# Attention, gated MLP and routed experts on one core: where the write of the converted expert weights stands in GpSimd's queue

## The chip, the cores and the metric

The kernel runs on one core of a Trainium2 chip, in one launch. The time is device time in microseconds (us) from the first to the last instruction with what lies around them; 1202.6 us is the median of three runs of the kernel before (1199.43, 1202.60 and 1203.38 us).

## The reference

Three stages in a row. First a two-sided attention, for each of 8 batch items and 8 heads, between 512 text rows `x` and 32 `state` rows of 64 features: softmax(x stateᵀ/8) state, softmax(state xᵀ/8) x. The two results are laid end to end to 8 x 544 = 4352 rows of 512 features. Second a gated MLP over these rows:

```
x = (sigmoid(x @ w_gate) * (x @ w_val)) @ w_out        # 512 -> 1536 -> 512
```

Third a router with 8 experts: each row goes to the expert with the largest logit, `out = p * (relu(x @ w1[e]) @ w2[e])`, 512 -> 1024 -> 512, where p is the softmax probability of that expert.

The MLP's weights arrive as 64-bit floats, the rest as 32-bit floats. The kernel carries a 32-bit value as a pair of 16-bit floats, a high part and a low part (value minus high part), and makes a product of pairs with three matmuls. So every operand has to be scaled by a power of two and split.

## The kernel before, in words

**Stages.** After a prologue (weights converted, attention of the first item) `token_block(b)` runs for the eight batch items b = 0 to 7. Each has a *gated part*: for the 12 feature groups fc of 128, `gate_val` (L657) makes 24 matmuls of 512 columns (L665 to L667; 12 for the gate, 12 for the value), ScalarE takes the sigmoid into the buffer `g` (L671), VectorE multiplies it by the value half (L673), ScalarE casts it to the high part (L678), and GpSimd subtracts to get the low part (L679, "the last subtraction of gated values"). `g` has two buffers, so the sigmoid of group fc+2 has to wait for the subtraction of group fc. The gate and value sums take two of four PSUM buffers for each group. Then comes the *down-projection part*: `mlp_out` for four tiles of 128 rows, 36 matmuls each (L722 to L724). The state rows follow as a ninth block, and then the expert tiles.

**Halves.** Work of other kinds is woven into a block at 36 places, `mid()` (L1153), called halves here: two for each group of the gated part (1 to 24: the odd one between the gate matmuls and the value matmuls, the even one behind the subtraction), three for each tile of the down-projection (25 to 36). At each half `mid()` runs what `todo` lists for it, and in most halves one step of a background generator. What `todo` lists is attention steps of the next item, routing steps, loads, and at halves 24, 26, ... 34 `state_weights(b + 1, m)`: small matmuls (L483) whose result M is taken out of PSUM by ScalarE (L490) and VectorE (L491), twice each.

**The background steps.** From b = 1 to 7 the generator is `conv_experts` (L594). It converts 64 pieces of the experts' weights, 128 x 1024 floats each: load into one of three buffers (L611, SyncE's queue), absolute sum with ScalarE ("bound", L617), spread of that over the partitions with a small matmul (L199, operand `em`), scale (VectorE), split into high and low part by `pair` (high part ScalarE L318, low part VectorE L319) into `out`, a tile with two buffers, and a write of `out` to the DRAM tensor `w_d` (L650), issued on GpSimd's queue. A piece takes three steps: step one is `pair(n)`; step two is the bound of piece n+1 and the write of piece n-1; step three is the load of n+3 and the scale of n+1. Each block runs 28 steps (halves 1 to 24 without every third, and 25 to 36), 196 in all. `pair(n+2)` uses the buffer that the write of piece n empties, and it stands two steps behind that write.

**Order.** The order of PE's instructions is the order of the program text. The order of the other engines' instructions is made ahead of the run by a planner that plays the program through with its own estimates of durations; each engine then runs its queue strictly in that order, whatever the chip's real times. `tc.issue_after(ins)` adds an edge to the plan: instructions of the block that run on the engine of `ins` are placed behind it in that engine's queue. It adds no wait. `behind()` (L217) applies it for the dictionary `last`: `last["A"]` and `last["D"]` are the newest sigmoid or M eviction on ScalarE and the newest multiplication, M eviction or row result on VectorE; `last["P"]` is the newest subtraction L679 on GpSimd, written down but not used.

**Others on GpSimd.** The scatter of routed rows (L825, each waits for the one before to have landed), the low parts of attention (L316), a mask product (L251).

Of the kernel before, what the change touches and what calls it, by code (L numbers as in the profile page):

```python
# [26 lines left out]
def attention_moe_router_kernel(  # L27
# [102 lines left out]
    def tl(shape, dt=F32, name="t", bufs=None, pool=None):  # L130
        kw = {} if bufs is None else {"bufs": bufs}
        return (pool or tiny).tile(shape, dt, name=name, tag=name, **kw)
# [81 lines left out]
    last = {}  # L214

    @contextmanager
    def behind():  # L217

        with ExitStack() as pins:
            for k in "AD":  # L220
                if k in last:
                    pins.enter_context(tc.issue_after(last[k].ins))
            yield

    def state_load(b):

        st = att.tile([P, H // 2, D], F32, name="st", tag="st", bufs=1)
        sv = state[b].rearrange("(c r h) s d -> h s c r d", h=2, c=NU)
        for i in range(2):
            for c in range(NU):  # L230
                for h in range(2):
                    k = 64 * i + NS * (h ^ c)
                    nc.sync.dma_start(out=st[k:k + NS, NP * c:NP * c + NP], in_=sv[h, :, c])
        states[b] = {"st": st}

    def state_max(b):

        g = states[b]
        m = tl([P, 1], name="sgm")
        nc.vector.tensor_reduce(  # L240
            m, g["st"].rearrange("p r d -> p (r d)"), axis=AX.X, op=ALU.max,
            apply_absolute_value=True,
        )
        yield
        r = all_max(spread(m), "sgr")
        g["s"], g["i"] = pow2_scale(r, 14, "sg", bufs=3)

        bf = att.tile([64, H // 2, 2, D], F32, name="bf", tag="a")
        bd = att.tile([64, 2, H // 2, 2, D], F16, name="bd", tag="sT")
        bsh = [64, H // 2, 2, D]  # L250
        nc.gpsimd.tensor_tensor(  # L251
            bf, g["st"][0:64].unsqueeze(2).to_broadcast(bsh),
            hmask[0:64].unsqueeze(3).to_broadcast(bsh), op=ALU.mult,
        )
        bw = bd.rearrange("p l r i d -> p l (r i d)")
        pair(bf.rearrange("p r i d -> p (r i d)"), bw[:, 0], bw[:, 1], g["s"][0:64])
        g["bd"] = bd
        yield

    def state_turn(b):  # L260

        g = states[b]
        bv = g.pop("bd").rearrange("p l r i d -> p l r (i d)")
        pb = at_ps([P, 2, H // 2, 64], F16)
        for l in range(2):
            for r in range(H // 2):
                nc.tensor.transpose(pb[:, l, r], bv[:, l, r], ident[0:64, 0:64])
        g["bdT"] = att.tile([P, 2, H // 2, 64], F16, name="bdT", tag="bdT")
        nc.vector.tensor_copy(g["bdT"], pb)

    def unit_load(n):

        if n >= NUN:
            return
        b, c = divmod(n, NU)
        u = units[n] = {}
        if n == 1:
            u["xb"] = big([P, HU, NJ, D])
        else:
            u["xb"] = att.tile([P, HU, NJ, D], F32, name="xb", tag="xb", bufs=1)  # L280
        for h in range(HU):
            nc.sync.dma_start(
                out=u["xb"][:, h],
                in_=x[b, HU * c + h].rearrange("(p j) d -> p j d", j=NJ),
            )

    def unit_max(n):

        if n >= NUN:
            return  # L290
        u, g = units[n], states[n // NU]
        m = tl([P, 1], name="uxm")

        junk = att.tile([P, NJ * HU * D], F16, name="xj", tag="aq")
        nc.scalar.activation(
            junk, u["xb"].rearrange("p h j d -> p (h j d)"), AF.Abs, accum_out=m
        )
        yield
        r = all_max(spread(m), "uxr")
        u["s"], i = pow2_scale(r, 14, "ux")  # L300

        for nm in ("c1", "c2", "c3", "n1"):
            u[nm] = tl([P, 1], name="s" + nm, bufs=3)
        nc.vector.tensor_scalar(u["c1"], i, g["i"], SCALE, ALU.mult, ALU.mult)
        nc.vector.tensor_scalar(u["n1"], u["c1"], -1.0, None, ALU.mult)
        nc.vector.tensor_scalar(u["c2"], u["c1"], 2.0 ** SC_SH, None, ALU.mult)
        nc.vector.tensor_scalar(u["c3"], i, 2.0 ** -PR_SH, None, ALU.mult)
        yield
# [786 lines left out]
    def token_block(b):  # L1095
        isig = states[b]["i"]
        acts = []
        sg = tl([P, NFC], name="sgf")
        todo = {}

        def at(slot, f):
            todo.setdefault(slot, []).append(f)

        if b + 1 < B:
            if b == 0:
                for u, slots in ((state_max(1), (13, 15)), (unit_max(NU), (14, 16))):
                    for slot in slots:
                        at(slot, lambda u=u: next(u, None))
            at(2 if b else 19, lambda: state_turn(b + 1))

            def first_step(n):
                gens[n] = att_unit(n)
                next(gens[n])

            for c in range(NU):
                n = NU * (b + 1) + c
                slots = (UNIT0, UNIT1)[b][c] if b < 2 else UNIT[c]
                if slots[0]:
                    at(slots[0], lambda n=n: first_step(n))
                for slot in slots[1:]:  # L1120
                    at(slot, lambda n=n: next(gens[n], None))
                if LOAD[min(b, 2)][c]:
                    at(LOAD[min(b, 2)][c], lambda n=n: unit_load(n + 1))
                um = unit_max(n + 1)
                for slot in UMAX[min(b, 2)][c]:
                    at(slot, lambda um=um: next(um, None))
            if 1 <= b < B - 2:
                at(EARLY, lambda: first_step(NU * (b + 2)))
                at(EARLY + 2, lambda: unit_load(NU * (b + 2) + 1))
            for m in range(NFP):  # L1130
                at(GV + 2 * m, lambda m=m: state_weights(b + 1, m))
        if b + 1 == B:
            rs = state_rows()
            at(6, lambda: next(rs, None))
            at(12, lambda: next(rs, None))
        if b + 2 < B:
            at(1 if b else 21, lambda: state_load(b + 2))
            sm = state_max(b + 2)
            at(9 if b else 30, lambda: next(sm, None))
            at(12 if b else 33, lambda: next(sm, None))  # L1140
        if b == 0:

            rw = router_weights()
            for slot in (25, 26, 27, 28, 29, 30, 31, 33):
                at(slot, lambda: next(rw, None))
        for slot in (35, 36) if b == 0 else ROUTE:
            at(slot, lambda: next(router[b], None))
        if b == 1:
            for slot in (3, 6):
                at(slot, lambda: next(router[0], None))  # L1150
        half = [0]

        def mid():  # L1153
            half[0] += 1
            with behind() if b else ExitStack():
                for f in todo.get(half[0], ()):
                    f()
                if half[0] > 12 if b == 0 else half[0] > GV or half[0] % 3:
                    pump(bg)

        if b > 0:
            nc.vector.tensor_scalar(
                sg, inv_w[:, 0], isig, 2.0 ** (M_SH - PR_SH), ALU.mult, ALU.mult
            )
        for fc in range(NFC):
            if b == 0 and fc % 2 == 0:
                fp = fc // 2
                state_weights(0, fp)
                nc.vector.tensor_scalar(
                    sg[:, fc:fc + 2], inv_w[:, 0, fc:fc + 2], isig, 2.0 ** (M_SH - PR_SH),  # L1170
                    ALU.mult, ALU.mult,
                )
                if fp + 2 < NFP:
                    cvs[fp + 2] = conv_wgv(fp + 2, raws.pop(fp + 2))
                    next(cvs[fp + 2])
                    if fp + 3 < NFP:
                        raws[fp + 3] = load_wgv(fp + 3)
            elif b == 0 and fc // 2 + 2 < NFP:
                drain(deque([cvs.pop(fc // 2 + 2)]))
            gate_val(fc, S, sg, V_SH, token_chunks(b, fc), acts, mid)  # L1180
        if b == 0:
            drain(bg)
        rt_new(b, isig)
        router[b] = route(b, NJ, acts)
        for j in range(NJ):
            mlp_out(NJ * b + j, j, acts, mid)
        if b == 0:
            bg.append(ce)
# [279 lines left out]
```

## Time and profile before

| what | value |
|---|---|
| median of three runs | 1202.6 us |
| the profiled execution: its time, its span | 1203.0 us, 1201.3 us |
| PE busy, share of the span | 1077.0 us, 90% |
| VectorE busy | 858.8 us, 71% |
| ScalarE busy | 560.1 us, 47% |
| GpSimd busy | 310.1 us, 26% |
| writes of w_d issued on GpSimd (L650) | 63 (a 64th at L656), 35.5 us in all |
| subtractions L679 | 108, 138.7 us in all |

How to read it: the blocks 1 to 7, in which the expert weights are converted, run from about 223 to 752 us. Each is some 75 us long, the first half of it the gated part. A share over the whole span mixes these with the prologue (before 215 us) and the expert tiles (after 790 us). In a timeline row the figures are start, duration, engine, line, what is written and read, and in brackets the idle time of the engine just before, with what ended it.

### The profile page before, as it was taken

What the parts mean: (1) busy time and instruction counts of PE and PEld (TensorE: products, weight loads), DVE (VectorE), ACT (ScalarE), POOL (GpSimd) and SP (SyncE); (2) the same over time, 40 slices, a digit from 0 to 9 for tenths busy, and PEclk for the clock granted to TensorE, in tenths of its full rate; (3) what the DMA queues carried; (4) which work ended last, traced back from release to release, by engine and by line L of the source; (5) the groups of instructions that cost most, each with busy time, mean ns of one, the idle gap of its engine ahead of it and who ended that gap; (6) DMA issues with size and microseconds to landing.
All of it is one profiled execution on the core that took longest, in us unless ns stands there. A gap on an engine that the chain in (4) does not pass through costs nothing. (4 is left out here: it accounts for less than half of the span.)

```text
span 1201.3 us, 22322 instructions
## 1 busy us (share of the span) xinstructions
PE 1077.0 (90%) x8303; PEld 589.6 (49%) x8303; DVE 858.8 (71%) x2079; ACT 560.1 (47%) x967; POOL 310.1 (26%) x305
## 2 busy tenths in 40 slices
PE   2265659889899999999999999999999999999997
PEld 1221224434344444344444444867666667776674
DVE  6878996688787887887877765447656666565564
ACT  3566563774776857767678483311111111111111
POOL 1244310350532524415235071301100000000000
PEclk9576779999999999999999999999999999999999
DMA  7422566545756667557465652473312495979348
GB/s 254 162 71 88 158 114 120 124 162 140 218 168 176 224 142 216 167 159 237 121 207 158 159 195 95 139 232 120 88 42 50 109 357 127 312 248 366 81 82 292
DMA packets 187745, 200.65 MB, mean 167 GB/s; under 512 B 130159, under 2 KB 154735, under 8 KB 184304
## 3 DMA queue, kind: packets, MB, share of 16 engines
q1 hardware_dynamic: 172736, 147.51, 45.0%
q0 software_dynamic: 14896, 51.67, 11.3%
q8 instruction: 67, 1.10, 0.4%
q14 instruction: 46, 0.38, 0.1%
HBM read 217.40 MB, written 54.88 MB: 227 GB/s over the span
## 5 line engine op out<-in xcount | busy, mean ns | idle before, releaser
L910 ACT CAST acth<-v 128x256 f16<-128x256 f32 x148 | 59.9, 404 | 331.2 <-DVE v L909 308.3
L679 POOL TENSOR_TENSOR actl<-g,acth 128x512 f16<-128x512 f32 (+1 forms) x108 | 138.7, 1286 | 161.8 <-ACT acth L678 161.3
L665 PE MATMUL mm<-aT,M 128*128 128x512 f16 x384 | 152.8, 398 | 26.1 <-ACT M L490 19.9
L722 PE MATMUL mm<-wout,acth 128*128 128x512 f16 x408 | 156.2, 383 | 9.1 <-DVE wout L590 8.8
L667 PE MATMUL mm<-aT,M 128*128 128x512 f16 x384 | 152.2, 396 | 11.5 <-DVE M L491 11.5
L723 PE MATMUL mm<-wout,acth 128*128 128x512 f16 x408 | 156.0, 382 | 0.0
L724 PE MATMUL mm<-wout,actl 128*128 128x512 f16 x408 | 155.8, 382 | 0.0
L666 PE MATMUL mm<-aT,M 128*128 128x512 f16 x384 | 152.7, 398 | 0.0
L895 PEld LDWEIGHTS <-wgv 128*128 128x128 f16 x1184 | 115.6, 98 | 20.0 <-DMA wgv<-w_d 2.8
L924 POOL DMA_INDIRECT out_dram<-g,meta x37 | 35.9, 972 | 344.5 <-DVE g L921 286.7
L895 PE MATMUL mm<-big,wgv 128*128 128x256 f16 x704 | 118.5, 273 | 1.5 <-DMA wgv<-w_d 1.5
L898 PEld LDWEIGHTS <-wgv 128*128 128x128 f16 x1184 | 115.8, 98 | 3.8
L898 PE MATMUL mm<-big,wgv 128*128 128x128 f16 x704 | 117.4, 219 | 0.0
L908 DVE TENSOR_REDUCE v<-mm 128x256 f32<-128x512 f32 x148 | 101.4, 685 | 19.8 <-PE mm L898 18.8
L911 DVE TENSOR_TENSOR actl<-v,acth 128x256 f16<-128x256 f32 x148 | 62.8, 424 | 68.6 <-ACT acth L910 68.6
L319 DVE SCALAR_TENSOR_TENSOR out<-big,inv,out 128x1024 f16<-128x1024 f32 x64 | 83.5, 1305 | 36.7 <-ACT out L318 36.7
L673 DVE SCALAR_TENSOR_TENSOR g<-mm,g 128x512 f32<-128x512 f32 (+1 forms) x108 | 70.9, 657 | 53.3 <-PE mm L667 27.3
L318 ACT ACTIVATE out<-big,inv 128x1024 f16<-128x1024 f32 x64 | 73.2, 1144 | 52.6 <-DVE inv L140 45.5
L671 ACT ACTIVATE g<-mm,sgf 128x512 f32<-128x512 f32 (+1 forms) x108 | 71.2, 660 | 43.5 <-POOL actl L679 26.4
L650 POOL DMA_DIRECT2D w_d<-out x63 | 35.5, 563 | 189.3 <-DVE out L319 138.1
L678 ACT CAST acth<-g 128x512 f16<-128x512 f32 (+1 forms) x108 | 63.3, 588 | 40.8 <-DVE g L673 40.6
L895 PE MATMUL mm<-out,wgv 128*128 128x256 f16 x480 | 80.8, 273 | 0.0
(320 smaller groups left out, 2152.3 us busy)
## 6 DMA issues: line engine op xcount, KB each, us to landing
wgv<-w_d SPq DMA_DIRECT2D x56, 2048.0 KB
wout<-w_d SPq DMA_DIRECT2D x18, 2048.0 KB
big<-in_moe_w_dram SPq DMA_DIRECT2D x64, 512.0 KB
w_d<-out POOLq DMA_DIRECT2D x64, 512.0 KB, 4.9
xb<-in_x_dram SPq DMA_DIRECT2D x60, 128.0 KB
wgv<-in_moe_w_gate_dram SPq DMA_DIRECT2D x3, 1024.0 KB
wgv<-in_moe_w_val_dram SPq DMA_DIRECT2D x3, 1024.0 KB
wout<-in_moe_w_gate_dram SPq DMA_DIRECT2D x3, 1024.0 KB
```

The source lines that it names most:

```text
L318: nc.scalar.activation(h16, v, AF.Copy, scale=s)
L319: nc.vector.scalar_tensor_tensor(l16, v, s, h16, op0=ALU.mult, op1=ALU.subtract)
L665: nc.tensor.matmul(ps[k], w[0], v[0], start=(i == 0), stop=False)
L666: nc.tensor.matmul(ps[k], w[0], v[1], start=False, stop=False)
L667: nc.tensor.matmul(ps[k], w[1], v[0], start=False, stop=(i == len(parts) - 1))
L679: last["P"] = nc.gpsimd.tensor_tensor(lo, g, h, op=ALU.subtract)
L722: nc.tensor.matmul(po, hj, wout[:, fc, 1], start=(fc == 0), stop=False)
L723: nc.tensor.matmul(po, hj, wout[:, fc, 0], start=False, stop=False)
L724: nc.tensor.matmul(po, lj, wout[:, fc, 1], start=False, stop=(fc == NFC - 1))
L895: nc.tensor.matmul(ph[:, i], w1s[:, pr, c, 0, f], t[:, :, c], start=(c == 0), stop=False)
L898: nc.tensor.matmul(ph[:, i, 1], w1s[:, pr, c, 1, f], t[:, 0, c], start=False, stop=(c == NDC - 1),)
L908: nc.vector.tensor_reduce(v, ph.rearrange("p i l q -> p i q l"), axis=AX.X, op=ALU.add)
```

## The change

`behind` takes the names of the engines whose newest instruction pins the block, and `mid` uses it twice: with "AD" around the listed work, as before, and anew with "ADP" around the background step. So in blocks 1 to 7 what a step issues on GpSimd (the write L650) is placed behind the newest subtraction L679 of the text above it. Because the second `with` is entered after the listed work has been written down, its "A" and "D" are also newer in halves that list `state_weights`: there they are the M evictions of that same half.

```
     @contextmanager
-    def behind():
+    def behind(names):
 
         with ExitStack() as pins:
-            for k in "AD":
+            for k in names:
                 if k in last:
                     pins.enter_context(tc.issue_after(last[k].ins))
             yield
...
         def mid():
             half[0] += 1
-            with behind() if b else ExitStack():
+            with behind("AD") if b else ExitStack():
                 for f in todo.get(half[0], ()):
                     f()
+            with behind("ADP") if b else ExitStack():
                 if half[0] > 12 if b == 0 else half[0] > GV or half[0] % 3:
                     pump(bg)
```

## Rows read from the trace of the kernel before

**Rows 1.** Busy time by stage, gated parts of blocks 1 to 7; columns as headed

```profile
core 0: us, PE busy (x) PEld busy (x) DVE busy (x) ACT busy (x) POOL busy (x), PEclk, DMA share, GB/s
...
301.00:340.00 39.00, 34.38 (x201) 15.22 (x200) 30.21 (x73) 31.11 (x49) 21.45 (x21) 1.00 0.74 220
...
sum 260.00, PE 242.45 PEld 107.90 DVE 197.35 ACT 212.09 POOL 154.75; mean PE 34.64 PEld 15.41 DVE 28.19 ACT 30.30 POOL 22.11
```

**Rows 2.** The same view, the seven down-projection parts

```profile
sum 269.00, PE 268.48 PEld 120.98 DVE 220.93 ACT 149.30 POOL 44.18; mean PE 38.35 PEld 17.28 DVE 31.56 ACT 21.33 POOL 6.31
```

**Rows 3.** PE's waits, 223 to 752 us: for whom, total us, times, longest

```profile
PE at L199 <- ACT junk L617: 7.8, 6, 2.4
PE mm L665 <- ACT g L671: 5.9, 4, 2.5
PE at L199 <- DVE uxr L206: 3.0, 2, 1.7
PE at L199 <- ACT xj L295: 0.3, 1, 0.3
```

**Rows 4.** ScalarE's waits in the same stretch

```profile
ACT g L671 <- POOL actl L679: 26.4, 18, 3.3
```

**Rows 5.** The write's line: durations in ns, and us from issue to landing

```profile
L650 POOL DMA_DIRECT2D w_d<-out x63: 531/561/617, 230.8 to 744.4; - x63
...
DMA to landing us min/median/max: 2.9/4.9/6.6
```

**Rows 6.** GpSimd's timeline in the gated part of block 2

```profile
317.52 0.58 POOL L650 DMA_DIRECT2D w_d<-out  x1
318.11 2.60 POOL L679 TENSOR_TENSOR actl<-g,acth 128x512 f16<-128x512 f32 x2
322.88 0.58 POOL L650 DMA_DIRECT2D w_d<-out  x1 [2.17 <-DVE out L319]
...
329.86 1.18 POOL L679 TENSOR_TENSOR actl<-g,acth 128x512 f16<-128x512 f32 x1 [3.20 <-ACT acth L678]
```

**Rows 7.** ScalarE's timeline in the same part

```profile
319.45 0.69 ACT L671 ACTIVATE g<-mm,sgf 128x512 f32<-128x512 f32 x1 [1.36 <-POOL actl L679]
...
329.69 1.15 ACT L318 ACTIVATE out<-big,inv 128x1024 f16<-128x1024 f32 x1
```

**Rows 8.** PE's timeline in the same part

```profile
320.19 0.38 PE L665 MATMUL mm<-aT,M 128*128 128x512 f16 x1 [1.91 <-ACT g L671]
...
327.11 0.23 PE L199 MATMUL at<-identb,em 128*128 128x128 bf16 x1 [2.42 <-ACT junk L617]
```

**Rows 9.** VectorE's timeline in the same part

```profile
321.32 1.27 DVE L319 SCALAR_TENSOR_TENSOR out<-big,inv,out 128x1024 f16<-128x1024 f32 x1
322.51 0.68 DVE L673 SCALAR_TENSOR_TENSOR g<-mm,g 128x512 f32<-128x512 f32 x1
```

**Rows 10.** First and last late buffer, GpSimd's timeline

```profile
230.81 0.62 POOL L650 DMA_DIRECT2D w_d<-out  x1
...
243.28 1.19 POOL L679 TENSOR_TENSOR actl<-g,acth 128x512 f16<-128x512 f32 x1
...
715.13 0.57 POOL L650 DMA_DIRECT2D w_d<-out  x1
...
719.90 1.17 POOL L679 TENSOR_TENSOR actl<-g,acth 128x512 f16<-128x512 f32 x1
```

**Rows 11.** First and last late buffer, ScalarE's timeline

```profile
248.59 1.14 ACT L318 ACTIVATE out<-big,inv 128x1024 f16<-128x1024 f32 x1
...
721.21 1.14 ACT L318 ACTIVATE out<-big,inv 128x1024 f16<-128x1024 f32 x1
```

**Rows 12.** Half 26 of block 1, ScalarE's timeline

```profile
262.64 1.06 ACT L617 ACTIVATE junk<-big 128x1024 fp8e5<-128x1024 f32 x1
...
266.97 1.08 ACT L490 ACTIVATE M<-mm 128x512 f16<-128x512 f32 x2
```

**Rows 13.** The spread matmul behind it, PE's timeline

```profile
268.21 0.23 PE L199 MATMUL at<-identb,em 128*128 128x128 bf16 x1
```

More of the change, by code (lines that the diff above doesn't have):

```diff
@@ L216, in behind @@
     @contextmanager
-    def behind():
+    def behind(names):
         with ExitStack() as pins:
-            for k in "AD":
+            for k in names:
                 if k in last:
@@ L1154, in mid @@
             half[0] += 1
-            with behind() if b else ExitStack():
+            with behind("AD") if b else ExitStack():
                 for f in todo.get(half[0], ()):
                     f()
+            with behind("ADP") if b else ExitStack():
                 if half[0] > 12 if b == 0 else half[0] > GV or half[0] % 3:
```

## The prediction

> **What bounds the kernel now.** I read the busy times by stage first. In the seven down-projection parts PE is busy 268.5 of 269 us [rows 2]: nothing there can become faster by an order of other engines, only slower. In the seven gated parts it is busy 242.45 of 260 us [rows 1], so 17.5 us stand open over all blocks. That is the most that an edit of queues in blocks 1 to 7 can win; outside of them the program is untouched. Next the waits of PE name what these 17.5 us are [rows 3]: 7.8 us for a "bound" of the experts' weights on ScalarE, 5.9 us for a sigmoid that empties PSUM, 3.0 us for a reduction of the next text's maximum on VectorE. Two of the three end on ScalarE, which is itself busy 212.1 of 260 us in these parts [rows 1] and has 47.9 us idle there. Part of that idle time is 26.4 us in which a sigmoid waits for the subtraction on GpSimd that frees its buffer `g` [rows 4]. So the chain to look at is: subtraction, sigmoid, PSUM, PE; GpSimd is in it, and what is issued ahead of a subtraction there delays it.
>
> Then I went through GpSimd's timeline write by write, and counted for each write how many subtractions stand above it in the program text and how many had run ahead of it. Of the 63 writes of L650, 43 run ahead of one to three subtractions that stand above them; the other 20 belong to the down-projection, where the last subtraction is long done. Rows 6 show one: the write at 322.88 us is that of half 16 of block 2, so eight subtractions stand above it, and the eighth begins at 329.86 us. The planner takes the write early because its data are ready and the subtraction is not.
>
> **The change part by part.**
>
> *The write leaves its place ahead of the subtractions.* An issue costs GpSimd 0.56 us [rows 5]. In 15 of the 43 cases a subtraction starts straight behind it with no other wait, so at most 15 x 0.56 = 8.4 us of delay go on GpSimd. What PE sees of it is less: the write at 317.52 us ends in the subtraction at 318.11, for whose end (the first of the two, 319.41) the sigmoid at 319.45 waits [rows 6, 7], and for that the matmul at 320.19 [rows 8]. Here 0.6 us come off the path. Elsewhere the subtraction waits for a scatter, or PE has no wait on a sigmoid. With 0.4 us for the few shorter waits of that kind I take -1.0 us; the ends are 0 and -5.9 us, all of PE's waits for a sigmoid [rows 3].
>
> *The write comes later, and so does its buffer.* This is the cost. Moving each of the 43 behind the subtraction that it now has to follow, and leaving all else where it is, puts them later by 7.4 us in the mean. `out` has two buffers, and an issue lands after 2.9 to 6.6 us, median 4.9 [rows 5]. The write of 322.88 us goes to the end of the subtraction at 331.04 us [rows 6] and lands at 335.9; the high part of the piece after next, which needs that buffer, starts today at 329.69 us [rows 7]: 6.2 us late. The same sum for all 62 writes with a successor gives 29 late ones, 96.5 us together, ten of them over 4 us; the first is 244.5 + 4.9 - 248.6 = 0.8 us, the last 721.1 + 4.9 - 721.2 = 4.8 us [rows 10, 11]. With 2.9 us to landing it would be 22 and 42 us, with 6.6 us 32 and 148 us. In the trace of before no high part waits for a landing at all, so this is a new wait. Behind the waiting high part in ScalarE's queue stand sigmoids, casts and the next bound; for the sigmoid waits PE (PSUM), for the cast GpSimd, for the bound PE again (the spread matmul has a fixed place). On SyncE the load of the piece three further on waits for the buffer that this one reads, and the next text's loads and transposes queue behind that load.
>
> What of the 96.5 us is paid? Nothing (0), if the planner, which knows that the buffer is taken, puts other work in front. All that ScalarE's idle time does not swallow, 96.5 - 47.9 = 48.6 us, if the order stays. I take the part that a planner cannot know, the spread of the landing: 6.6 - 4.9 = 1.7 us on 29 places is 49 us; PE stands today at 13 of the 7 x 12 = 84 feature groups [rows 3], so a delay there reaches it in 15%, 7.6 us; half of the landings come before the median: +3.8 us.
>
> The Trainium skill ("DMA: Bandwidth & Descriptors", the section on the anatomy of a GpSimd-issued DMA) gives 2.0 us plus the bytes over 436e3 per us, which for 512 KB makes 3.2 us, an estimate by that page. The write here takes 4.9 us in the median [rows 5], so the trace does not agree. By the page 25 high parts would be late by 49 us together, and halving the term would put the sum 1.9 us lower.
>
> *VectorE's order.* In block 2 the low part at 321.32 us stands in front of the multiplication at 322.51 us [rows 9], which is in the chain that ends in PE's 2.42 us wait for a bound [rows 8]. A high part held back by a late buffer takes its low part with it, and the multiplication can go 1.2 us earlier. Block 5 has the same pattern. I count one of the two: -1.2 us, ends 0 and -2.4.
>
> *The newer pins for "A" and "D".* In halves 26, 28, ... 34 the step now stands behind the M evictions of its own half. Ten bounds stand in such halves. The bound of half 26 in block 1 runs at 262.64 us, the M evictions end at 268.05 [rows 12]; behind them the bound ends at 269.1, and the spread matmul that needs it starts today at 268.21 [rows 13]: PE waits 0.9 us. Block 4 repeats this with some 0.6 us; the other eight bounds still end before their matmul, by 0.2 us or more. Term: +1.5 us, ends 0 and +4 (half a microsecond more on the tight ones). PE has no slack there [rows 2], so it is paid in full. In return M leaves PSUM earlier in some halves, which wins nothing, as PE does not wait for it.
>
> *Sum.* -1.0 + 3.8 - 1.2 + 1.5 = +3.1 us on the profiled execution's 1203.0 us, 1206.1 us. The median of the three runs is 0.4 us below that execution, so 1205.7 us is what I expect to be measured.
>
> **The rivals.**
>
> *A. Absorbed.* The planner puts the late high parts into ScalarE's idle time and nothing of it reaches PE. For it: 47.9 us idle in the gated parts, and the high part itself is needed by nobody until its write. Against it: the planner has its own durations, and its subtractions may run earlier than the real ones, which wait for scatters. Time: -1.0 - 1.2 + 1.5 = about -0.7 us, 1202 us.
>
> *B. The cleared path.* With writes and high parts out of the way, sigmoid, cast and subtraction follow each other more closely, and bounds overtake high parts. PE's waits for ScalarE and for the maximum, 16.7 us [rows 3], halve: -8.4 + 1.5 = -6.9 us, some 1196 us. For it: the 15 subtractions straight behind a write, and 26.4 us of sigmoids waiting for GpSimd. Against it: from block 4 on PE waits for no sigmoid any more, so most of these 26.4 us are off the path today.
>
> *C. Slower: the write's turn becomes a loop.* A high part waits at ScalarE's head for a landing, the sigmoid behind it comes late, so does its subtraction, and the next write, pinned to it, lands later still. It decides once a sigmoid stands directly behind a waiting high part more than twice in a block. Price: a third of the 48.6 us, +16 us, 1219 us. For it: the ten places over 4 us. Against it: only one write comes every 2.25 feature groups, some 7.5 us, so a delay can run out before the next.
>
> That the edge does not act on the write is possible as well; the time would then be that of A without its first two terms, and it is counted there.
>
> **How the numbers follow.** What a measurement of this kernel can tell from no change is 0.3%, 3.6 us: 1199.0 to 1206.2 us. The forecast gets 0.42: its own range, from the ends of its small terms, is 1201 to 1212, and 0.23 of it lies above 1206.2, 0.19 within. A gets 0.24 (0.21 within, 0.02 faster, 0.01 slower), B 0.23 (0.21 faster, 0.02 within), C 0.11, all slower. Together: faster 0.23, same 0.42, slower 0.35. The range takes in B's value and C's: 1195 to 1218 us.
>
> **What would show each step.** On GpSimd, every write of L650 in blocks 1 to 7 behind the subtraction that stands above it, and no subtraction straight behind a write of an earlier group; the 26.4 us of sigmoids waiting for GpSimd smaller. On ScalarE, waits of L318 for the landing of w_d, absent today: none would speak for A, many of 1 to 3 us for the forecast, many with a sigmoid right behind for C. On PE, the wait for L617 in the gated parts bigger than 7.8 us by the forecast, smaller by B; a new wait of about 1 us at the spread matmul of half 27 in blocks 1 and 4 by the last term. Busy time of PE by part: down-projection parts unchanged within 2 us, the gated parts longer. The prediction is wrong if the gated parts together become shorter by more than 4 us, or if the time is lost in the state rows or the expert tiles, which I take as untouched.

## The result and the profile after

The change makes the kernel slower: 1216.0 us median (1212.1 to 1222.7, 6 runs) against 1198.8 us (1193.7 to 1203.4, 6 runs), a ratio of 1.0149, 95% interval 1.0107 to 1.0191, or +17.3 us. The profiled execution of the kernel before (span 1201.3 us) lies some 4 us above that kernel's median, so the two traces differ by less than the medians: 1215.4 - 1201.3 = 14.1 us of span.

First the busy time by stage, on the kernel after, with the parts at their new places: the gated parts of blocks 4 and 5 and the sum of all seven, then the sum of the seven down-projection parts. Columns are as in rows 1.

```profile
461.00:501.00 40.00, 35.51 (x205) 15.79 (x202) 29.61 (x78) 31.31 (x49) 21.44 (x20) 0.96 0.64 187
543.00:590.00 47.00, 39.03 (x210) 16.56 (x210) 29.50 (x85) 34.81 (x56) 22.89 (x21) 0.93 0.56 160
...
sum 269.00, PE 238.81 PEld 106.11 DVE 188.43 ACT 212.17 POOL 145.71; mean PE 34.12 PEld 15.16 DVE 26.92 ACT 30.31 POOL 20.82
...
sum 276.00, PE 273.07 PEld 123.00 DVE 225.46 ACT 151.24 POOL 47.05; mean PE 39.01 PEld 17.57 DVE 32.21 ACT 21.61 POOL 6.72
```

PE's idle time in the gated parts grew from 17.5 us [rows 1] to 269.0 - 238.8 = 30.2 us, that in the down-projection parts from 0.5 us [rows 2] to 2.9 us: 15.1 us together, which is the difference of the spans within 1 us. ScalarE's busy time in the gated parts is the same as before (212.2 against 212.1 us); nothing was added, it was placed otherwise.

Then what PE waited for in the blocks, on the kernel after (total us, times, longest):

```profile
PE at L199 <- ACT junk L617: 11.4, 7, 2.8
PE at L362 <- DMA xT<-xn: 6.7, 3, 4.1
PE at L381 <- DVE uxr L206: 6.4, 2, 3.2
PE mm L665 <- ACT g L671: 5.4, 3, 3.3
PE at L199 <- DVE uxr L206: 1.7, 2, 1.3
PE at L199 <- ACT xj L295: 1.4, 2, 0.7
```

Against rows 3 two waits are new: 6.7 us for the transposed text `xT`, which SyncE's transposing DMA brings, and 6.4 us at the transposition of the scores (L381). The waits for a bound rose by 3.6 us. The wait for a sigmoid, which the pin could have shortened, went from 5.9 to 5.4 us.

ScalarE's waits and the write's own line on the kernel after answer to rows 4 and 5:

```profile
ACT g L671 <- POOL actl L679: 25.6, 20, 3.7
ACT out L318 <- DMA w_d<-out: 15.8, 8, 4.8
```

```profile
L650 POOL DMA_DIRECT2D w_d<-out x63: 531/552/612, 244.9 to 760.7; - x63
...
DMA to landing us min/median/max: 2.9/4.1/8.8
```

Sigmoids still wait 25.6 us for GpSimd (26.4 before). The high parts now wait for a landing, eight times and 15.8 us. And a write that took at most 6.6 us to land takes up to 8.8 us, though the median fell. (Not every landing is in a trace. The longest of the eight waits, 4.8 us, is for a write issued 9.7 us earlier.) Block 4 shows what goes with this, on SyncE, GpSimd, ScalarE and PE in this order:

```profile
479.09 4.15 SPq L341 DMA_TRANSPOSE xT<-xn  x1
```

```profile
479.98 0.56 POOL L650 DMA_DIRECT2D w_d<-out  x1
```

```profile
488.78 1.15 ACT L318 ACTIVATE out<-big,inv 128x1024 f16<-128x1024 f32 x1 [2.91 <-DMA w_d<-out]
```

```profile
489.01 1.49 PE L362 MATMUL at<-xT,bdT 128*64 128x512 f16 x6 [4.14 <-DMA xT<-xn]
```

The pinned write starts 0.9 us behind the transpose of the same block's second unit, and the two are ready for their readers within 0.3 us of each other: the write lands 8.8 us behind its issue, the matmul that reads the transpose starts 9.9 us behind that one's. ScalarE stands for the one, PE for the other. In the kernel before the write nearest to this transpose starts 4.8 us behind it, neither is waited for, and the reader starts 8.2 us behind the transpose's issue.

The second new wait, L381, is in blocks 2 and 5 and comes through VectorE's queue. On the kernel after in block 5: ScalarE, then VectorE, then PE.

```profile
579.97 1.15 ACT L318 ACTIVATE out<-big,inv 128x1024 f16<-128x1024 f32 x1
```

```profile
581.15 1.83 DVE L319 SCALAR_TENSOR_TENSOR out<-big,inv,out 128x1024 f16<-128x1024 f32 x1 [2.14 <-ACT out L318]
582.91 0.68 DVE L673 SCALAR_TENSOR_TENSOR g<-mm,g 128x512 f32<-128x512 f32 x1
583.51 0.27 DVE L206 TENSOR_REDUCE uxr<-at 128x1 f32<-128x128 f32 x1
```

```profile
583.84 0.71 PE L381 MATMUL at<-ident,sT 128*128 128x128 f16 x8 [3.21 <-DVE uxr L206]
```

VectorE stands 2.1 us idle at the low part, which has to wait for its high part, and the reduction behind it in the queue, which PE needs, comes late. The high part itself does not wait for a landing here: its row has no idle time in front.

### The profile page after: what moved, and what is told of

Its sections match the earlier page's. It is cut to its first block, busy times and chain, and to the rows that moved or that the text cites. A ratio compares the mean times of both kernels' runs of the same rounds, so it can differ in the third digit from the quotient of the medians.

```text
span 1215.4 us, 22276 instructions
## 1 busy us (share of the span) xinstructions
PE 1077.5 (89%) x8303; PEld 590.0 (49%) x8303; DVE 855.0 (70%) x2079; ACT 562.3 (46%) x967; POOL 305.0 (25%) x305
## 5 line engine op out<-in xcount | busy, mean ns | idle before, releaser
L679 POOL TENSOR_TENSOR actl<-g,acth 128x512 f16<-128x512 f32 (+1 forms) x108 | 133.3, 1237 | 200.2 <-ACT acth L678 199.5
L671 ACT ACTIVATE g<-mm,sgf 128x512 f32<-128x512 f32 (+1 forms) x108 | 71.2, 660 | 40.6 <-POOL actl L679 25.6
L490 ACT ACTIVATE M<-mm 128x512 f16<-128x512 f32 x96 | 52.1, 591 | 61.8 <-PE mm L483 61.8
```

Of the source, the lines that this page charges most:

```text
L679: last["P"] = nc.gpsimd.tensor_tensor(lo, g, h, op=ALU.subtract)
```

## Experiments

Theory 1 was that of the prediction: the cost is the lateness of the `out` buffers. Theory 2 came from the traces of the first four runs: the moved writes meet the transposing DMA, and both land late. (The next item's attention runs as two units of four heads; in the second one, the transpose of the text is issued at half 13 of a block.) The rivals stand in the expectations.

**e1: the newer pins for ScalarE and VectorE alone.**

```
-            with behind("ADP") if b else ExitStack():
+            with behind("AD") if b else ExitStack():
```

> Only the newer pins for ScalarE and VectorE (the step behind the M evictions of its own half); GpSimd is not pinned. Theory 1 (the loss comes from the write being held back on GpSimd): +1 to +3 us over before, in the down-projection parts of blocks 1 and 4, no wait of L318 for a landing of w_d; ratio 1.001 to 1.003. Rival (the newer pins make the loss, the GpSimd pin is harmless): +13 to +18 us, 1.011 to 1.015.

Measured 1201.3 us, ratio 1.0019 (0.9999 to 1.0038). On its trace, half 26 of block 1, ScalarE and PE:

```profile
267.12 1.08 ACT L490 ACTIVATE M<-mm 128x512 f16<-128x512 f32 x2
268.08 1.06 ACT L617 ACTIVATE junk<-big 128x1024 fp8e5<-128x1024 f32 x1
```

```profile
269.28 0.23 PE L199 MATMUL at<-identb,em 128*128 128x128 bf16 x1 [1.14 <-ACT junk L617]
```

The bound now stands behind the M evictions, and PE waits 1.1 us at the place and of about the size worked out from rows 12 and 13. In block 4 it is 0.9 us, and a bound in block 3's down-projection part, with a high part now in front of it, costs 0.4 us. So some 2 us of the loss may be the newer pins; the interval allows 0 to 5.

**e2: the pin on GpSimd alone.** The pins are noted ahead of the listed work and used for the step with "P" added:

```
+            pin = [last[k] for k in "ADP" if k in last]
...
-            with behind("ADP") if b else ExitStack():
+            with behind(pin) if b else ExitStack():
```

> Only the pin on GpSimd, with the older pins for ScalarE and VectorE of the kernel before. Theory 1: +12 to +16 us over before, all of it in the gated parts; L318 waits 10 to 20 us for landings of w_d; no new wait in the down-projection parts of blocks 1 and 4. Rival (newer pins): 0 to +3 us.

Measured 1221.2 us, ratio 1.0191 (1.0155 to 1.0228): the pin alone costs at least as much as the whole change. PE's wait for xT is 9.1 us in three places, the longest 6.9 us; the wait at L381 is 6.4 us; the high parts wait 15.7 us for landings. The loss of 21.8 us is more than the 12 to 16 us expected; the rival is out.

**e3: as e2, the pin one subtraction older.**

```
+        subs.append(nc.gpsimd.tensor_tensor(lo, g, h, op=ALU.subtract))
+        last["P"] = subs[max(0, len(subs) - 2)]
```

> As the pin alone, but behind the subtraction one feature group older. Moved in the trace of before, the lateness of the buffers falls from 96.5 to 22.6 us (29 to 16 pieces). Theory 1 (cost follows the lateness): +2 to +5 us. Rival (any new order of the plan costs this much, whatever the lateness): +10 us or more. Rival (it is the issue behind a subtraction as such): as with the full pin.

Measured 1210.6 us, ratio 1.0111 (1.0076 to 1.0146). Less than the full pin, but +11 us where theory 1 had +2 to +5: the mark of the first rival (any new order costs 10 us or more) is met, here and in e4. Against it speak e7 and e10, new orders that cost 3 to 4 us. The waits for landings are 5.0 us, those for xT 2.9 us, those at L381 6.8 us.

**e4: the write two steps earlier in the program, pinned.**

```
             bound(n + 1)
-            if late:
-                nc.gpsimd.dma_start(out=late[0], in_=late[1])
-            late = dst, o
             yield
             load(n + 3)
             scale(n + 1)
+            nc.gpsimd.dma_start(out=dst, in_=o)
             yield
```

> The whole change, but each write stands two steps earlier in the program (in the third step of its own piece), so its pin is a subtraction 1.5 groups older. Lateness worked out on the trace of before: 4.2 us (9 pieces) where the change has 96.5. Theory 1: the loss goes down to the +1 to +3 us of the newer pins, L318 hardly waits for landings (under 3 us). Rival (new order as such): +10 us or more.

Measured 1214.9 us, ratio 1.0122 (1.0086 to 1.0158). This refutes theory 1 as the whole cause: almost no buffer was due late, and the loss stayed. Its trace names what was lost, first PE's waits, then ScalarE's:

```profile
PE at L362 <- DMA xT<-xn: 13.3, 3, 6.9
```

```profile
ACT out L318 <- DMA w_d<-out: 10.1, 3, 5.1
```

The wait at L381 is gone here and the wait for xT has doubled. Both big ones stand where a write starts 0.6 or 0.3 us behind a transpose. I then listed, in the traces of the change and of e2 to e4, every transpose of a second unit and the writes around it. Eleven have a write 0.3 to 1.3 us behind their start. At ten of the eleven PE waits for xT, or ScalarE for the write, or both; PE's part is 27.9 of the 32.0 us that these four kernels wait for xT. In the kernel before and in e1 no write starts in that stretch behind a second unit's transpose, and PE never waits for one.

Not each of the eleven is a late transpose. At seven the reading matmul starts 8.8 to 13.3 us behind the issue, with 26.4 us of waiting. In the change's block 3, with the write 1.3 us behind, it starts after 5.0 us: that wait of 1.5 us is an early reader. And in e4's block 4, with 0.8 us between them, the write lands in 5.9 us and nobody waits, so the distance alone does not decide it. First units' transposes have a write 0.4 and 1.1 us behind them in the kernel before too; their readers come some 13 us behind the issue, so whether those transposes were late does not show.

Behind a stall of this length the clock is low as well. e4's matmul at 576.9 us had waited 6.9 us; the granted clock in the stretch behind it was 0.63, a mixture of the levels 1.2 and 2.4 GHz (before: 1.00 in the same stretch of time). Behind the change's wait of 4.1 us it was 0.62 from 489 to 493 us. The row of e4, by which an estimate of the cost is 8 x 0.37 = 3 us more:

```profile
577.00:585.00 8.00, 8.00 (x28) 2.93 (x29) 3.61 (x6) 5.53 (x10) 2.30 (x2) 0.63 0.63 225
```

**m1: the meeting by itself.** A kernel with nothing but the two transfers, each started by one VectorE instruction:

```
def case(t, delay, w, ld):
    nc.vector.tensor_tensor(go, zero, c1.to_broadcast([P, 512]), op=ALU.add)
    nc.vector.tensor_copy(xn[:, 0:1], go[:, 0:1])
    if t:
        nc.sync.dma_start_transpose(out=xT, in_=xn)
    ...                       # ld: a load of 512 KB behind it
    for k in range(delay):
        nc.gpsimd.tensor_tensor(a, go if k == 0 else a, zero, op=ALU.subtract)
    if w:
        nc.gpsimd.tensor_copy(o[:, 0:1], (a if delay else go)[:, 0:1])
        nc.gpsimd.dma_start(out=w_d, in_=o)
    ...                       # ScalarE reads xT, VectorE overwrites o
```

> Leaves out the whole computation; output is zeros. It measures the disputed cost by itself: a transposing DMA of 128 x 2048 half-precision values on SyncE's queue (the size of xT<-xn), a 512 KB write on GpSimd's queue (the size of w_d<-out), each alone and together, the write 0, 2 or 5 GpSimd subtractions behind the start, and with a 512 KB load. Theory 2 (the moved writes meet the transposes, and both land late): alone each lands in 3 to 6 us; the write issued 0 to 3 us behind the transpose lands in 7 to 10 us, and the transpose 2 to 5 us later than alone. Rival (no mutual delay, the late landings come from the load traffic): together as alone, within 1 us, and later only with the load.

Its timeline has ScalarE reading xT (L73) and VectorE overwriting the buffer (L76), with their waits. First the transpose alone:

```profile
88.72 0.19 ACT L73 CAST c<-xT 128x1 f32<-128x1 f16 x1 [5.70 <-DMA xT<-xn]
```

Then the write alone, then both, the write 0.35 us behind the transpose:

```profile
90.72 0.53 POOL L71 DMA_DIRECT2D w_d<-o  x1 [0.30 <-POOL o L70]
...
93.70 0.16 DVE L76 CAST o<-zero 128x1 f16<-128x1 f32 x1 [3.40 <-DMA w_d<-o]
...
95.85 0.53 POOL L71 DMA_DIRECT2D w_d<-o  x1 [0.30 <-POOL o L70]
103.58 0.16 DVE L76 CAST o<-zero 128x1 f16<-128x1 f32 x1 [8.14 <-DMA w_d<-o]
103.84 0.19 ACT L73 CAST c<-xT 128x1 f32<-128x1 f16 x1 [9.70 <-DMA xT<-xn]
```

And the write 3.0 us behind the start of the transpose:

```profile
108.69 0.57 POOL L71 DMA_DIRECT2D w_d<-o  x1 [0.30 <-POOL o L70]
110.04 0.19 ACT L73 CAST c<-xT 128x1 f32<-128x1 f16 x1 [5.70 <-DMA xT<-xn]
...
111.72 0.16 DVE L76 CAST o<-zero 128x1 f16<-128x1 f32 x1 [6.08 <-DMA w_d<-o]
```

Alone the transpose is ready 5.7 us after its start signal, and the write's buffer is free 3.0 us after its issue. Together the transpose takes 9.7 us and the write 7.7 us. With 3.0 us between them each takes its own time again (5.7 us; 108.69 to 111.72 us), and 5 subtractions behind as well. With 1.6 us between them, and a load besides, the transpose lands in 4.3 us as alone, the write in 5.0 to 5.3 us, which is also what it takes beside a load without a transpose. All six repetitions agree within 0.3 us. So the mutual delay is real, it is 4 to 5 us for each, and in this small kernel it appears only when they start nearly together. The expectation of a delay at 0 to 3 us is met at 0.35 us alone and missed at 1.6 and 3.0; nothing in between was measured. The stretch in the full kernel is somewhat wider (0.3 to 1.3 us); there the issue of the transpose on SyncE alone takes 2 to 4 us, here 1.3 us in the case together. Also, the full kernel issues four loads of the next text (128 KB each) on SyncE straight ahead of these transposes in blocks 1 to 5, which this case lacks; its longest, 13.3 us from issue to reader, goes beyond the 8.3 us here.

**e5 and e6: xT made on PE, without and with the change.**

```
-        if by_dma:
-            nc.sync.dma_start_transpose(
-                out=xT.rearrange("p l j r q -> p (l j r) q"),
-                in_=xn.rearrange("p l j h d -> p (l j h d)"),
-            )
-        for r in range(0 if by_dma else NP):
+        for r in range(NP):
```

> Control for the next run: the kernel before with the transposition xT<-xn made on PE in all blocks instead of by the transposing DMA. It adds 16 small transposes to PE and two copies to ScalarE and VectorE for each of 14 units: +5 to +25 us over before by every theory.

> The whole change, with xT<-xn made on PE as in the control, so that no write can meet that transpose. Theory 2 (the meeting is most of the loss): slower than the control by 2 to 8 us, instead of the 14 to 17 us of the change. Theory 1 (lateness of the buffers alone): slower than the control by 12 us or more.

Measured 1225.9 us (1.0226, 1.0185 to 1.0267; a little above the 5 to 25 us expected) and 1223.7 us (1.0197, 1.0160 to 1.0235). Without that transposing DMA the change costs nothing that can be told: 2 us less, well within the two intervals. On e6's trace ScalarE still waits for landings:

```profile
ACT out L318 <- DMA w_d<-out: 9.5, 11, 1.9
```

Eleven short waits instead of eight with up to 4.8 us, and the medians show no cost of them. Two reservations. The base is 27 us slower and its ScalarE and VectorE carry two more copies for each unit, so something of the change's cost could hide behind that. And PE does not go free: against e5 its wait for a bound rises from 3.1 to 8.7 us and that of L381 (L376 there) from 0.6 to 4.5 us, while other waits of e5 (5.1 us for the cast xn, its largest) are gone in e6.

**e7, e8, e9, e10: the transpose moved.** One edit, on top of e4 (e7), of before (e8), of the change (e9) and of e4 with the older pins of e2 (e10):

```
-    UNIT = ((0, 2, 8, 13, 24, 27, 28, 33), (9, 13, 19, 23, 25, 30, 32, 36))
+    UNIT = ((0, 2, 8, 13, 24, 27, 28, 33), (9, 11, 19, 23, 25, 30, 32, 36))
```

> The write two steps earlier and pinned (that run lost 15 us, 13.3 us of it at PE waiting for xT<-xn), with the attention step that issues the second unit's transpose moved from half 13 to half 11 of blocks 2 to 6. Theory 2: the writes of half 13 in blocks 2 and 5 no longer fall on the transpose, PE's wait for xT<-xn goes from 13.3 us to under 4 us and the loss from 15 to 3 to 8 us. Rival (the transpose is late for another reason, such as SyncE's queue): the wait stays.

Measured 1202.4 us, ratio 1.0026 (1.0006 to 1.0046). The loss of e4 goes from 15 to 3 us with this one number. On its trace no write starts 0.3 to 1.3 us behind a second unit's transpose, PE has no wait for xT any more and ScalarE none for w_d; the wait at L381 is 3.7 us. Two writes start 2.4 us behind such a transpose and land in 4.1 and 4.5 us, where the two of e4 took 8.9 and 9.6. The trace is of the fastest of the ten executions (1196.9 us).

> Control for e7, and a candidate of its own: the kernel before with only the second unit's transposing step at half 11 in place of 13 of blocks 2 to 6. If the earlier transpose were a gain by itself, this would be faster than before by 5 us or more, and e7's recovery would be that gain; by theory 2 it has nothing to recover here: -3 to +3 us.

Measured 1198.2 us, ratio 0.9990 (0.9964 to 1.0016): the earlier transpose is no gain of its own, so e7's recovery is a loss of e4's taken away. The edit does one thing more, though: at half 11 the transpose is issued ahead of the four loads of the next text, at half 13 straight behind them. Those loads alone do not make it late, for the kernel before has them there too, and in blocks 2 to 5 its matmuls start 6.6 to 8.2 us behind the transpose's issue without a wait. Whether the write meets the transpose alone or both with the loads, e7 and e9 do not separate.

> The whole change with the transposing step at half 11. By theory 2 the time follows from where the writes fall: of those of half 10 (block 3 and 6), 11 (2 and 5) and 13 (4) some still fall on the transpose. If PE's wait for xT<-xn is under 2 us the loss should be under 8 us, if it stays above 5 us the loss should be 12 us or more. Theory 1 (lateness of the buffers): the loss stays at 14 to 17 us in either case.

Measured 1208.6 us, ratio 1.0087 (1.0055 to 1.0118). The nearest writes start 0.8 us ahead or 2.8 us and more behind the transposes, and PE has no wait for xT. The loss falls from 17 to 10 us: past the 8 us that the expectation set, yet not the 14 to 17 of theory 1. So of the change's own loss the meeting accounts for some 7 us, and the larger part stays without it. What stays by its trace are PE's wait at L381 and ScalarE's for landings:

```profile
PE at L381 <- DVE uxr L206: 5.7, 2, 3.2
```

```profile
ACT out L318 <- DMA w_d<-out: 6.4, 5, 2.3
```

> As e7 but with the older pins for ScalarE and VectorE, which e1 showed to be some 2 us cheaper: 0 to 3 us below e7, so within 2 us of before; a version that beats both kernels if it goes well.

Measured 1202.5 us, ratio 1.0034 (1.0013 to 1.0056). The older pins give nothing back here, against the expectation. No version beats the kernel before.

## Why the prediction came out as it did

Its range held the time, and slower was allowed 0.35 against 0.23 for faster, but most, 0.42, went to no change, and the forecast of +3.1 us was a fifth of the +17.3 us. That the time lies within the range is owed to rival C's value, which widened it: the forecast's own range ended at 1212 us. By the mechanism that is luck. Rival C's 1219 us lies near the result, by its size and not by its mechanism: C needed a sigmoid right behind a waiting high part more than twice in a block, and there are eight waits in seven blocks in all.

*The step that failed* is the term for the later write: "I take the part that a planner cannot know, the spread of the landing: 6.6 - 4.9 = 1.7 us on 29 places ... +3.8 us". It carried the landing times of the old places [rows 5] over to the new ones. A landing time is not a property of the write here (2.9 us alone in m1, up to 12.6 us in e2); it depends on what else is on its way. The prediction did name the transposes, but as queued behind a load on SyncE, not as a transfer that the moved write runs into. What it measured: on the change's trace 6.7 us of PE's waiting for xT, where the prediction had none, 5.2 us of it at two stretched transposes, with a low clock behind one of them; by the runs of e9 some 7 us. e4 and e7 show this by putting it in and taking it out; m1 shows that the two transfers delay each other. What the rest of the +17.3 us is stays open. Named are 6.4 us at L381, which the prediction did not have either, and 3.6 us more for a bound: 2.9 us of its 11.4 are the two waits of the newer pins, and the longest, 2.8 us, stands in block 7, where the kernel before has one wait of 0.9 us.

*Late buffers* were predicted rightly as a new wait, 29 places and 96.5 us with nothing else moved; eight of them came, 15.8 us, and part of that is the stretched landings. What they cost by themselves stays open: in e6 eleven of them cost no time that the medians show, as rival A said, while e9 has five of them, 6.4 us, and is 10 us slower than before.

*VectorE's order* was given -1.2 us. The idea that a late high part lets the multiplication past was wrong in sign: in blocks 2 and 5 the low part keeps its place in VectorE's queue, the engine stands at it, and the 6.4 us at L381 follow. That this wait comes from the late buffers is not shown, and the runs speak against a simple tie: e4 has 10.1 us of waits for landings and no wait at L381, e7 and e10 have none of the former and 3.7 us of the latter. e9 keeps 5.7 us of it without any late transpose. Before, e1 and e8, which have no pin on GpSimd, do not have it. No run takes it away alone.

*The freed GpSimd* was given -1.0 us. Sigmoids wait 25.6 us for it instead of 26.4, PE 5.4 instead of 5.9 us for sigmoids: a gain of half a microsecond at most.

*The newer pins* were given +1.5 us in half 26 of blocks 1 and 4. e1 measures +1.9 us with an interval that takes in zero, and PE's wait there is 1.1 us in place of the 0.9 worked out. In the change's trace 2.9 us of PE's idle time in down-projection parts lie in those of blocks 1 and 4, half in each. This step was right.

*The page of the Trainium skill* that was weighed ("DMA: Bandwidth & Descriptors", anatomy of a GpSimd-issued DMA) gives an estimate of 3.2 us for 512 KB. m1 measures 2.9 to 3.0 us for the write alone: for a DMA alone page and trace agree within 0.3 us. The 4.9 us of rows 5 are nearer to m1's write beside a load, 5.0 to 5.3 us. The same page (issuing engines are not separate DMA queues) says that DMAs of all issuing engines run on the same 16 DMA engines and interleave. m1's 7.7 and 8.3 us to landing of write and transpose, issued 0.35 us apart, against 2.9 and 4.3 alone, agree with that.

*Open.* e9 loses 10 us by its runs, its profiled execution only 1205.1 - 1201.3 = 3.8 us of span; likewise e3 (11 and 7 us). The difference is the profiled execution of the kernel before, 4.6 us above that kernel's median beside e9, and e9's own, 1.8 us below its median. So the waits read from single traces do not add up to the losses by the medians. Whether transfers meet in some executions and not in others was not shown, and that a transpose 1.6 us ahead is no longer disturbed has no explanation here.

## What to carry to other kernels

When a DMA's issue is moved, even by an edge of order that adds no wait, look up which other transfers start at its new time before carrying its landing time over, transposing DMAs above all: in m1 both consumers then waited longer than the two transfers take one after the other (7.7 and 8.3 us against 2.9 + 4.3). A pin behind the "last" instruction of an engine ties a transfer to a phase of the loop; that it then meets the same neighbour again and again is an inference (four of the change's six blocks from 1 to 6 have a write within 1.3 us behind the transpose). And when a delay is removed and the loss stays, as in e4, the waits by name tell more than the model that was right about the delay.

## What the runs showed of the hardware

A transposing DMA of 512 KB lands in 4.3 us alone and in 8.3 us if a plain 512 KB write starts 0.35 us behind it; the write lands in 2.9 us alone and in 7.7 us then. At 1.6 us between the starts (beside a load), 3.0 and 7.0 us the transpose is not delayed. While the two share the DMA engines, the same bytes take more of the engines' time. Three stretches of m1 show it: the transpose alone, the write alone, both together. (Columns: from and to, us, busy VectorE, ScalarE and GpSimd, granted clock, DMA share, GB/s.)

```profile
84.00:89.00 5.00, 0.29 (x2) 0.28 (x2) 0.00 (x0) 1.00 0.56 105
90.00:94.50 4.50, 0.72 (x5) 0.19 (x1) 0.71 (x2) 1.00 0.30 118
95.00:104.50 9.50, 0.68 (x4) 0.48 (x3) 0.72 (x2) 1.00 0.63 110
```

Share times length is 2.8 and 1.4 us alone, 4.2 us in all, and 6.0 us together, at 1.05 MB either way. The full kernel has no such pair of rows: from 562 to 572 us the change's trace has a DMA share of 1.07 (booked twice in places) at 199 GB/s with a transpose on its way, the kernel before 0.75 at 260 GB/s, but there no transpose is issued in that stretch.
